# Three of 48 output weight rows spread over eight of the sixteen DMA engines, and score sums over two chunks at a time

## The chip, the cores and the metric

The kernel runs on one core of one Trainium2 chip. The metric is the device time of one execution in microseconds (us). All times below are in us unless they are marked ns. Engines are named as in the profile: PE is the matrix engine (PEld its weight loads), DVE the vector engine, ACT the scalar engine, POOL or GpSimd the general engine, SP the engine that issues most of the transfers. Sixteen DMA engines move the data between HBM and on-chip memory.

## What is computed

One decoding step of a transformer block with attention and a gated FFN side by side, for 4 batch rows (D = 640, 32 heads of Dh = 192, a window of W = 2048 of 8192 cached positions, F = 1536), in bf16:

```python
xn = layernorm(x)
q = (xn @ wq).reshape(B, 1, 32, 192)                   # wq: 640 x 6144
k, v = k_cache[:, :, -2048:, :], v_cache[:, :, -2048:, :]
p = softmax(q . k * 192 ** -0.5)
attn = (p . v).reshape(B, 1, 6144) @ wo                # wo: 6144 x 640
ffn = (silu(xn @ w1) * (xn @ w3)) @ w2                 # w1, w3: 640 x 1536; w2: 1536 x 640
out = x + attn + ffn
```

The windows of the two caches are 201 MB of the 223 MB that are read.

## The kernel before

The 128 partitions hold 32 heads times R = 4 groups of positions. Each batch row has 4 units of 512 positions, and each unit of keys or values is one load of 6,144 KB (`load`, 48 KB in each partition) into one of three `kv` buffers. All large loads are issued by SP in program order; each waits until the buffer that it overwrites is free. `feed` issues the next load of `stream` after each unit of work. Value units of row b alternate with key units of row b + 1.

*A key unit* (`keys`) has NC = 4 chunks of CH = 32 positions. `mult` (L212) multiplies a chunk with the query on DVE into one of two `pr` buffers; `adder` (L219) sums over 12 slices of Dh on PE with 12 matmuls by the identity into a PSUM tile of one bank (`ps_add`, two buffers); `reduces` (L229) sums the last 16 on DVE, one instruction for each chunk, 64 in all. `chain` then makes the softmax weights. *A value unit* (`values`) spreads the weights over heads on DVE (L268) and multiplies with the values in 64 matmuls (L280) into `o_ps` (two buffers). `evict` (L288) and `sort` (L296, L298) bring the result of a batch row into `oT`, with Dh split as 4 x 48: row i of 48 in each partition.

*The end.* wo is used as 48 rows of 640 for each of the 128 partitions (`A_wo.rearrange("(p i) n -> p i n", i=48)`). `wo_load` (L307) loads rows 38 to 47 into a `pr` buffer, then rows 0 to 25 and 26 to 37 into a `kv` buffer, with all partitions at once. `proj` (L315) makes two matmuls for each row, all into one accumulator `acc`: first rows 38 to 47, then 0 to 37. The weights of the FFN's first half (w1, w3) are loaded and used before; w2 comes last, in three pieces of 8, 3 and 1 rows (`w2_load`, L329), and its 24 matmuls (L423) follow the projection. DVE adds `x_st` (the input, loaded by two tiny GpSimd transfers, L125) and `acc`, then the FFN's result (L426), and two transfers write the output. `ordered` fixes the order of instructions on PE and DVE. PSUM has 8 banks: 2 for `ps_add`, 2 for `ps_o`, 3 for `ps_t` (small results, FFN), 1 for `acc`. `pad` (ALIGN) only shifts the addresses of the tiles behind it.

Of the kernel before, what the change touches and what calls it, by code (L numbers as in the profile page):

```python
# [18 lines left out]
def kernel(  # L19
# [15 lines left out]
    WI: int = 10,  # L35
    WM: int = 26,
    ALIGN: int = 64,
):
# [7 lines left out]
    nc = tc.nc  # L46
# [35 lines left out]
    ps_add = ctx.enter_context(tc.tile_pool(name="ps_add", bufs=2, space=MemoryType.PSUM))  # L82
    ps_o = ctx.enter_context(tc.tile_pool(name="ps_o", bufs=2, space=MemoryType.PSUM))
    ps_t = ctx.enter_context(tc.tile_pool(name="ps_t", bufs=3, space=MemoryType.PSUM))
    ps_acc = ctx.enter_context(tc.tile_pool(name="ps_acc", bufs=1, space=MemoryType.PSUM))
# [35 lines left out]
    nc.gpsimd.memset(x_st[:], 0.0)  # L121

    def x_load():
        for t in range(2):
            nc.gpsimd.dma_start(out=x_st[32 * t:32 * t + B, :], in_=x_rows[:, t * DH:(t + 1) * DH])  # L125
# [8 lines left out]
    for s in range(2):  # L134
        load("k", 0, s)

    idb = const.tile([P, P], BF16, name="idb")
# [18 lines left out]
    for b in range(B):  # L156
        nc.vector.tensor_copy(out=qwin[:, b, at:at + NG * R].rearrange("p (g r) -> p g r", r=R),
                              in_=idf[:, b:P:32].unsqueeze(2).to_broadcast([P, NG, R]))
    oT = const.tile([P, NI, 32], BF16, name="oT")
    nc.gpsimd.memset(oT[:], 0.0)  # L160
# [26 lines left out]
    q_pss = []  # L187
    for k in range(NH // 2):
        pool, tag = (ps_add, "ps") if k < 2 else (ps_o, "o_ps")
        qp = pool.tile([P, 512], FP32, tag=tag)  # L190
        q_pss.append(qp)
    for kc in range(KC):
# [8 lines left out]
    for b in range(B):  # L201
        bp = ps_t.tile([P, Dh], FP32, tag="t")
        for k in range(NH):
            w0 = (NH - 1 - k) * NG * R
            pe(nc.tensor.matmul(bp[:], lhsT=qwin[:, b, w0:w0 + P], rhs=q_sb[:, k, :], start=(k == 0), stop=(k == NH - 1)))  # L205
        nc.scalar.copy(out=qb[:, b, :], in_=bp[:])

    scs, es, rss, rcps, pend = {}, {}, {}, {}, []

    def mult(b, s, c):  # L210
# [3 lines left out]
        return pr  # L214

    def adder(b, s, c, pr):
        ps = ps_add.tile([P, CH, DD], FP32, tag="ps")
        for kk in range(NK):
            pe(nc.tensor.matmul(ps[:], lhsT=idb[:], rhs=pr[:, :, kk * DD:(kk + 1) * DD], start=(kk == 0), stop=(kk == NK - 1)))  # L219
        pend.append((b, s, c, ps))  # L220

    def reduces():
        while pend:
            b, s, c, ps = pend.pop(0)
            if b not in scs:
                sc = small.tile([P, NU * NJ], FP32, tag="sc", bufs=1)
                scs[b] = sc
            at = s * NJ + c * CH
            dve(nc.vector.tensor_reduce(out=scs[b][:, at:at + CH], in_=ps[:], axis=AX.X, op=ALU.add))  # L229

# [123 lines left out]

    proj0, proj1 = NI - WI, NI - WI - 1

    def last_values():
        for g in range(VS):
            load("v", B - 1, NU - 1, g * NJ // VS, (g + 1) * NJ // VS)
        wo_load((NI - WI, NI), ppool, "pr", [P, WI, D])  # L360

# [4 lines left out]
    def last_weights():  # L366
        wo_load((0, WM, NI - WI), kvpool, "kv", [P, NJ, Dh])
        for i0, i1 in ((0, (NF - 1) * CF), ((NF - 1) * CF, NF * CF - 1), (NF * CF - 1, NF * CF)):
            w2_load(i0, i1)
# [5 lines left out]
    stream = [(load, u) for u in units[2:-1]] + [(gates, ()), (last_values, ()), (last_weights, ())]  # L375

    def feed():
        fn, args = stream.pop(0)
        fn(*args)

    feed()
# [28 lines left out]
    sort(B - 1)  # L410
    proj(NI - WI, NI)
    proj(0, NI - WI)

# [45 lines left out]
```

## Time and profile before

| | us |
|---|---|
| median of 3 runs | 526.01 (525.87 to 526.31) |
| the profiled execution | 526.01 |
| its span in the profile | 524.08 |
| one unit of keys or values, issue to landing (median) | 28.2 / 27.3 |
| DVE product of one chunk, L212 x64 | 3.351 each, 213.4 in all |
| DVE sum of one chunk, L229 x64 | 0.687 each, 43.9 in all |
| PE adder, L219 x768 | 194.1 in all |
| PE values, L280 x1024 | 115.1 in all |
| PE projection, L315 x96 | 9.5 in all |
| DMA | 223.26 MB, 426 GB/s in the mean |

A page shows one profiled execution: busy time of each engine, its share in 40 slices of the span, the DMA queues, the chain of work that ended last, and the costliest groups of instructions. "L219 PE" is line 219 on PE; "out<-in" are the kernel's tile names. Packets of the trace are pieces that one DMA engine moves as a whole: q1 is the queue of SP's transfers, q0 that of GpSimd's, q8 and q14 are instruction fetches. Behind each engine's part of a transfer stands a completion packet of 4 bytes.

### The profile page before, as it was taken

The page shows a single profiled execution, that of the slowest core. Times are in us where ns is not written, and L with a number is a line of the kernel's source. Part 1 is how long each engine was busy: PE and PEld are TensorE (multiplying, and loading weights), DVE is VectorE, ACT ScalarE, POOL GpSimd, SP SyncE. Part 2 cuts the span into 40 slices and gives each one's busy share as a digit, 9 for nine tenths or more (in the row PEclk, how much of TensorE's full clock was granted, in tenths as well). Part 3 has the DMA queues.
Part 4 walks back from the last instruction along what each step waited for, and adds up shares of the span by engine and source line. Part 5 has one row for each costly group of instructions (what it writes and reads, how often), then busy time and mean ns, then how long its engine had stood idle before and what let it go on. Part 6 is the DMA issues. An engine that isn't in the chain of part 4 may idle for free.

```text
span 524.1 us, 4690 instructions
## 1 busy us (share of the span) xinstructions
PE 341.9 (65%) x2147; PEld 199.4 (38%) x2147; DVE 300.5 (57%) x189; ACT 17.8 (3%) x34; POOL 4.7 (1%) x13
## 2 busy tenths in 40 slices
PE   0507677667676776596675866686565867688447
PEld 0302233253524352363434342353324353475445
DVE  4018999876583937676564828675574839411200
ACT  2110000000000000000000000000000000001100
POOL 3000000000000000000000000000000000000000
PEclk9977999979897887889798887998797888888797
DMA  9999999999999999999999999999999999999995
GB/s 361 431 448 439 420 425 447 439 421 424 436 450 425 420 435 451 431 418 439 443 433 424 424 455 431 425 420 450 436 431 421 435 448 428 428 420 427 432 425 240
DMA packets 6299, 223.26 MB, mean 426 GB/s; under 512 B 756, under 2 KB 904, under 8 KB 1032
## 3 DMA queue, kind: packets, MB, share of 16 engines
q1 hardware_dynamic: 6200, 222.96, 98.6%
q8 instruction: 16, 0.26, 0.2%
q14 instruction: 3, 0.02, 0.0%
q0 software_dynamic: 64, 0.01, 0.0%
q10 hardware_dynamic: 16, 0.01, 0.0%
HBM read 222.96 MB, written 0.01 MB: 425 GB/s over the span
## 4 chain that ended last, share of the span: by engine, by line
DMA 43%; DVE 29%; PE 25%; issue 1%; ACT 1%; SPq 0%; DVEq 0%; ACTq 0%
DMA kv<-in_A_k_cache_dram 38%; DVE pr L212 21%; PE o_ps L280 12%; PE ps L219 9%; DMA wt<-in_A_wo_dram 6%; DVE z L268 4%; DVE sc L229 4%; PE acc L315 2%; PE fp L296 1%; ACT e L252 1%; PE ft L423 0%; PE mt L247 0%; DVE gmax L244 0%; DVE gmq L246 0%; PE mt L242 0%
## 5 line engine op out<-in xcount | busy, mean ns | idle before, releaser
L212 DVE TENSOR_TENSOR pr<-kv,qb 128x6144 bf16<-128x6144 bf16 x64 | 213.4, 3351 | 104.7 <-DMA kv<-in_A_k_cache_dram 104.7
L219 PE MATMUL ps<-pr,idb 128*128 128x512 bf16 x768 | 194.1, 409 | 96.8 <-DVE pr L212 96.8
L219 PEld LDWEIGHTS <-idb 128*128 128x128 bf16 x768 | 79.5, 104 | 208.6 <-issue 122.6
L280 PE MATMUL o_ps<-kv,z 128*64 128x384 bf16 x1024 | 115.1, 396 | 50.6 <-DVE z L268 45.4
L280 PEld LDWEIGHTS <-z 128*64 128x64 bf16 x1024 | 94.5, 197 | 70.6 <-DVE z L268 53.0
L229 DVE TENSOR_REDUCE sc<-ps 128x32 f32<-128x512 f32 x64 | 43.9, 687 | 47.3 <-PE ps L219 47.2
L268 DVE TENSOR_TENSOR z<-e,selz 128x4096 bf16<-128x4096 bf16 (+1 forms) x17 | 36.7, 2158 | 18.2 <-PE o_ps L280 14.5
L315 PE MATMUL acc<-wt,oT 128*32 128x320 bf16 x96 | 9.5, 371 | 6.7 <-DMA wt<-in_A_wo_dram 6.1
L415 DVE CAST t<-acc 64x320 bf16<-64x320 f32 x1 | 0.5, 483 | 22.3 <-PE acc L315 22.3
L288 ACT COPY o_ev<-o_ps 128x384 f32<-128x384 f32 x4 | 1.9, 479 | 289.5 <-PE o_ps L280 289.5
L196 PE MATMUL qp<-wq,xnT 128*32 128x384 bf16 x80 | 5.2, 440 | 7.9 <-DMA wq<-in_A_wq_dram 7.9
L315 PEld LDWEIGHTS <-oT 128*32 128x32 bf16 x96 | 6.5, 118 | 9.5 <-issue 7.0
L296 PEld LDWEIGHTS fp<-o_ev,esel 128*128 128x128 f32 x64 | 7.7, 192 | 1.3 <-ACT o_ev L288 0.9
L296 PE MATMUL fp<-o_ev,esel 128*128 128x48 f32 x64 | 7.6, 272 | 0.6 <-ACT o_ev L288 0.6
L344 DVE TENSOR_TENSOR t_bf<-sg,t_bf 96x512 bf16<-96x512 bf16 x1 | 0.4, 420 | 11.5 <-ACT t_bf L338 11.5
L180 PE MATMUL xnT_ps<-idb,scratch 4*128 4x4 bf16 x5 | 0.4, 178 | 9.9 <-DVE scratch L176 9.9
L196 PEld LDWEIGHTS <-xnT 128*32 128x32 bf16 x80 | 3.1, 128 | 9.8 <-issue 7.5
L252 ACT ACTIVATE e<-sc,negm 128x512 bf16<-128x512 f32 x4 | 2.9, 721 | 80.5 <-DVE negm L249 80.5
L259 DVE RECIPROCAL rcp<-tb 128x1 f32<-128x1 f32 x4 | 0.6, 160 | 7.4 <-PE tb L257 7.4
L298 ACT ACTIVATE oT<-fp,rcp 128x48 bf16<-128x48 f32 x4 | 1.9, 468 | 64.9 <-PE fp L296 64.9
L180 PEld LDWEIGHTS <-scratch 4*128 4x128 bf16 x5 | 0.3, 125 | 9.9 <-DVE scratch L176 9.9
L205 PE MATMUL bp<-scratch 128*128 128x192 bf16 x32 | 3.3, 245 | 0.3
(60 smaller groups left out, 48.1 us busy)
## 6 DMA issues: line engine op xcount, KB each, us to landing
kv<-in_A_k_cache_dram SPq DMA_DIRECT2D x16, 6144.0 KB, 28.2
kv<-in_A_v_cache_dram SPq DMA_DIRECT2D x15, 6144.0 KB, 27.3
wq<-in_A_wq_dram SPq DMA_DIRECT2D x1, 6144.0 KB, 17.4
kv<-in_A_v_cache_dram SPq DMA_DIRECT2D x2, 3072.0 KB
wt<-in_A_wo_dram SPq DMA_DIRECT2D x1, 4160.0 KB, 29.4
ft<-in_B_w_dram SPq DMA_DIRECT2D x2, 1920.0 KB, 18.2
wt<-in_A_wo_dram SPq DMA_DIRECT2D x1, 1920.0 KB
wt<-in_A_wo_dram SPq DMA_DIRECT2D x1, 1600.0 KB, 27.8
```

Source lines behind the costliest of these rows:

```text
L196: pe(nc.tensor.matmul(q_pss[k][32 * g:32 * g + 32, 0:QW], lhsT=xnT[:, kc, :], rhs=wq[:, 2 * k:2 * k + 2, g, :], start=(kc == 0), stop=(kc ...
L205: pe(nc.tensor.matmul(bp[:], lhsT=qwin[:, b, w0:w0 + P], rhs=q_sb[:, k, :], start=(k == 0), stop=(k == NH - 1)))
L212: dve(nc.vector.tensor_tensor(out=pr[:], in0=kvs["k", b, s][:, c * CH:(c + 1) * CH, :], in1=qb[:, b, :].unsqueeze(1).to_broadcast([P, CH, ...
L219: pe(nc.tensor.matmul(ps[:], lhsT=idb[:], rhs=pr[:, :, kk * DD:(kk + 1) * DD], start=(kk == 0), stop=(kk == NK - 1)))
L229: dve(nc.vector.tensor_reduce(out=scs[b][:, at:at + CH], in_=ps[:], axis=AX.X, op=ALU.add))
L252: nc.scalar.activation(out=e[:], in_=sc[:], func=ACTF.Exp, bias=negm[:, 0:1], scale=SCALE, accum_out=rs[:])
L268: dve(nc.vector.tensor_tensor(out=z[:].rearrange("p h (a j) -> p h a j", j=ZB), in0=es[b][:, at:at + n].rearrange("p (a j) -> p a j", j=ZB ...
L280: pe(nc.tensor.matmul(o_pss[b][64 * t:64 * t + 64, 0:2 * Dh], lhsT=zf[:, a:a + (2 * H - 1) * half + 1:half], rhs=vt[:, n0 + a:n0 + a + hal ...
L288: nc.scalar.copy(out=o_ev[:].rearrange("p t d -> p (t d)"), in_=o_pss.pop(b)[:, 0:2 * Dh])
L296: pe(nc.tensor.matmul(fp[:], lhsT=esel[:, t, R - 1 - c:R - 1 - c + P], rhs=o_ev[:, t, c * NI:(c + 1) * NI], start=(c == 0 and t == 0), sto ...
L298: nc.scalar.mul(out=oT[:, :, b:b + 1].rearrange("p i o -> p (i o)"), in_=fp[:], mul=rcps.pop(b)[:, 0:1])
L315: pe(nc.tensor.matmul(acc[32 * t:32 * t + 32, :], lhsT=oT[:, i, :], rhs=wos[i][:, t * DH:(t + 1) * DH], start=(i == i0 and i0 == proj0), s ...
```

## The change

WX = 3 of the 48 wo rows, 45 to 47, leave the common loads. They go into a tile of their own, `wx`, which is zeroed by GpSimd at the start. In `wx`, partitions 0 to 15 and 32 to 47 (of the lower half) and 80 to 95 and 112 to 127 (of the upper half) take the rows of two partitions each, their own and those of a partition 16 away; the other partitions stay zero. There are 16 loads of 4 partitions x 2 x 3,840 bytes. Eight, for the lower half, are issued by SP, one after each of eight unit loads (`feed`). Eight, for the upper half, are issued by GpSimd after the last copy of the query (`qcopy`), each behind a transfer `turn` of 12 partitions x 2 x 16 bytes whose data is not used. The first dimension of a row load is 4 and that of a turn is 12, by which each goes over as many DMA engines.

`proj_ends` computes with these rows: two matmuls by the constant `swap` put each partition's `oT` columns, its own and the other's, side by side (`xp`), ACT copies them to `oX`, and 12 matmuls add to `acc`. It stands between the projection of rows 35 to 44 and that of rows 0 to 34. The pieces of wo become rows 35 to 44, 0 to 22 and 23 to 34.

The adder's PSUM tile holds two chunks (two banks, two buffers), and `reduces` sums two chunks with one instruction, 32 in all. For these banks `ps_o` has one buffer instead of two and `ps_t` two instead of three. The query's four accumulators lie in two adder tiles. ALIGN is 192.

```diff
...
     CH: int = 32,
     R: int = 4,
     WI: int = 10,
-    WM: int = 26,
-    ALIGN: int = 64,
+    WM: int = 23,
+    WX: int = 3,
+    ALIGN: int = 192,
 ):
 
 
...
     opool = ctx.enter_context(tc.tile_pool(name="o", bufs=1))
     small = ctx.enter_context(tc.tile_pool(name="small", bufs=2))
     ps_add = ctx.enter_context(tc.tile_pool(name="ps_add", bufs=2, space=MemoryType.PSUM))
-    ps_o = ctx.enter_context(tc.tile_pool(name="ps_o", bufs=2, space=MemoryType.PSUM))
-    ps_t = ctx.enter_context(tc.tile_pool(name="ps_t", bufs=3, space=MemoryType.PSUM))
+    ps_o = ctx.enter_context(tc.tile_pool(name="ps_o", bufs=1, space=MemoryType.PSUM))
+    ps_t = ctx.enter_context(tc.tile_pool(name="ps_t", bufs=2, space=MemoryType.PSUM))
     ps_acc = ctx.enter_context(tc.tile_pool(name="ps_acc", bufs=1, space=MemoryType.PSUM))
 
     ORDER_DEP = mybir.DependencyInfo(mybir.DependencyClass.NoSync, mybir.DependencyReason.SCHED_ONLY)
...
     x_st = const.tile([64, DH], BF16, name="x_st")
     nc.gpsimd.memset(x_st[:], 0.0)
 
+    wx = const.tile([P, 2, WX * D], BF16, name="wx")
+    nc.gpsimd.memset(wx[:], 0.0)
+    wo_ends = A_wo.rearrange("(p i) n -> p i n", i=NI)[:, NI - WX:NI, :].rearrange("(y x h e q) i n -> y x q e h (i n)", y=2, x=2, h=2, e=4)
+    wx_rows = wx[:].rearrange("(y x h e q) h2 n -> y x h q e h2 n", y=2, x=2, h=2, e=4)
+
+    def wx_load(y, x, q, queue):
+        return queue.dma_start(out=wx_rows[y, x, y, q], in_=wo_ends[y, x, q])
+
     def x_load():
         for t in range(2):
             nc.gpsimd.dma_start(out=x_st[32 * t:32 * t + B, :], in_=x_rows[:, t * DH:(t + 1) * DH])
...
     nc.sync.dma_start(out=wq1[:], in_=wq_rows[:, RV:KC, :])
     for s in range(2):
         load("k", 0, s)
-
     idb = const.tile([P, P], BF16, name="idb")
     make_identity(nc, idb[:])
     idf = const.tile([P, P], FP32, name="idf")
...
     for b in range(B):
         nc.vector.tensor_copy(out=qwin[:, b, at:at + NG * R].rearrange("p (g r) -> p g r", r=R),
                               in_=idf[:, b:P:32].unsqueeze(2).to_broadcast([P, NG, R]))
+    swap = const.tile([P, 2, 4, 2, 16], BF16, name="swap")
+    for h in range(2):
+        nc.gpsimd.tensor_copy(out=swap[:, h], in_=idb[:].rearrange("p (a h r) -> p a h r", a=4, h=2)[:, :, h:h + 1, :].to_broadcast([P, 4, 2, 16]))
     oT = const.tile([P, NI, 32], BF16, name="oT")
     nc.gpsimd.memset(oT[:], 0.0)
 
...
     acc = ps_acc.tile([64, DH], FP32, name="acc")
 
     q_pss = []
-    for k in range(NH // 2):
-        pool, tag = (ps_add, "ps") if k < 2 else (ps_o, "o_ps")
-        qp = pool.tile([P, 512], FP32, tag=tag)
-        q_pss.append(qp)
+    for k in range(0, NH // 2, 2):
+        qp = ps_add.tile([P, 2, 512], FP32, tag="ps")
+        q_pss += [qp[:, 0, :], qp[:, 1, :]]
     for kc in range(KC):
         wq = (wq0[:, kc, :] if kc < RV else wq1[:, 0, :]).rearrange("p (k g d) -> p k g d", g=NG, d=Dh)
         for k in range(NH // 2):
...
         for k in range(NH):
             w0 = (NH - 1 - k) * NG * R
             pe(nc.tensor.matmul(bp[:], lhsT=qwin[:, b, w0:w0 + P], rhs=q_sb[:, k, :], start=(k == 0), stop=(k == NH - 1)))
-        nc.scalar.copy(out=qb[:, b, :], in_=bp[:])
+        qcopy = nc.scalar.copy(out=qb[:, b, :], in_=bp[:])
+    turn = const.tile([12, 8, 2, 8], BF16, name="turn")
+    behind_q = mybir.DependencyInfo(mybir.DependencyClass.Sync, mybir.DependencyReason.SCHED_ONLY)
+    for x in range(2):
+        for q in range(4):
+            di = ordered("pool", nc.gpsimd.dma_start(out=turn[:, 4 * x + q],
+                                                     in_=A_wo.rearrange("(p i) n -> p i n", i=NI)[0:12, 4 * x + q:4 * x + q + 2, 0:8]))
+            if x == 0 and q == 0:
+                tc.add_manual_dep(di.ins, qcopy.ins.name, behind_q, reason="behind the short runs of the query weights")
+            ordered("pool", wx_load(1, x, q, nc.gpsimd))
 
     scs, es, rss, rcps, pend = {}, {}, {}, {}, []
 
...
                                     in1=qb[:, b, :].unsqueeze(1).to_broadcast([P, CH, Dh]), op=ALU.mult))
         return pr
 
+    adds = {}
+
     def adder(b, s, c, pr):
-        ps = ps_add.tile([P, CH, DD], FP32, tag="ps")
+        if c % 2 == 0:
+            ps = ps_add.tile([P, 2, CH, DD], FP32, tag="ps")
+            adds[b, s] = ps
+        ps = adds[b, s]
         for kk in range(NK):
-            pe(nc.tensor.matmul(ps[:], lhsT=idb[:], rhs=pr[:, :, kk * DD:(kk + 1) * DD], start=(kk == 0), stop=(kk == NK - 1)))
-        pend.append((b, s, c, ps))
+            pe(nc.tensor.matmul(ps[:, c % 2], lhsT=idb[:], rhs=pr[:, :, kk * DD:(kk + 1) * DD], start=(kk == 0), stop=(kk == NK - 1)))
+        if c % 2 == 1:
+            pend.append((b, s, c - 1, ps))
 
     def reduces():
         while pend:
...
                 sc = small.tile([P, NU * NJ], FP32, tag="sc", bufs=1)
                 scs[b] = sc
             at = s * NJ + c * CH
-            dve(nc.vector.tensor_reduce(out=scs[b][:, at:at + CH], in_=ps[:], axis=AX.X, op=ALU.add))
+            dve(nc.vector.tensor_reduce(out=scs[b][:, at:at + 2 * CH], in_=ps[:].rearrange("p a j d -> p (a j) d"), axis=AX.X, op=ALU.add))
 
     def keys(b, s):
         for c in range(NC):
...
             pe(nc.tensor.transpose(out=hT_ps[:, c, :], in_=ffn["h"][0:32 * NF, c:NCH:CF], identity=idb[0:32 * NF, 0:32 * NF]))
         dve(nc.vector.tensor_copy(out=hT[:], in_=hT_ps[:]))
 
-    proj0, proj1 = NI - WI, NI - WI - 1
+    NM = NI - WX
+    oX = const.tile([P, 2, WX, 32], BF16, name="oX")
+
+    def proj_ends():
+        xp = ps_t.tile([P, 2, WX * 32], FP32, tag="t")
+        for o in range(2):
+            pe(nc.tensor.matmul(xp[:, o, :], lhsT=swap[:, o].rearrange("p a h r -> p (a h r)"),
+                                rhs=oT[:, NM:NI, :].rearrange("p i o -> p (i o)"), start=True, stop=True))
+        nc.scalar.copy(out=oX[:].rearrange("p o i b -> p (o i b)"), in_=xp[:].rearrange("p o n -> p (o n)"))
+        for o in range(2):
+            for i in range(WX):
+                for t in range(2):
+                    at = i * D + t * DH
+                    pe(nc.tensor.matmul(acc[32 * t:32 * t + 32, :], lhsT=oX[:, o, i, :], rhs=wx[:, o, at:at + DH],
+                                        start=False, stop=False))
+
+    proj0, proj1 = NM - WI, NM - WI - 1
 
     def last_values():
         for g in range(VS):
             load("v", B - 1, NU - 1, g * NJ // VS, (g + 1) * NJ // VS)
-        wo_load((NI - WI, NI), ppool, "pr", [P, WI, D])
+        wo_load((NM - WI, NM), ppool, "pr", [P, WI, D])
 
     def gates():
         ffn_load(1)
         ffn_load(3)
 
     def last_weights():
-        wo_load((0, WM, NI - WI), kvpool, "kv", [P, NJ, Dh])
+        wo_load((0, WM, NM - WI), kvpool, "kv", [P, NJ, Dh])
         for i0, i1 in ((0, (NF - 1) * CF), ((NF - 1) * CF, NF * CF - 1), (NF * CF - 1, NF * CF)):
             w2_load(i0, i1)
 
...
             units += [("v", b, s)] + ([("k", b + 1, s)] if b < B - 1 else [])
     stream = [(load, u) for u in units[2:-1]] + [(gates, ()), (last_values, ()), (last_weights, ())]
 
+    ends = [(0, x, q, nc.sync) for x in range(2) for q in range(4)]
+
     def feed():
         fn, args = stream.pop(0)
         fn(*args)
+        if ends and len(stream) < len(units) - NU:
+            wx_load(*ends.pop(0))
 
     feed()
     for which, b, s in units[:-1]:
...
         values(B - 1, NU - 1, g * NJ // VS, (g + 1) * NJ // VS)
     evict(B - 1)
     sort(B - 1)
-    proj(NI - WI, NI)
-    proj(0, NI - WI)
+    proj(NM - WI, NM)
+    proj_ends()
+    proj(0, NM - WI)
 
     t1 = opool.tile([64, DH], BF16, tag="t1")
     dve(nc.vector.tensor_copy(out=t1[:], in_=acc[:]))
```

## The prediction

> **What bounds the kernel now.** I read the page from its first three parts to the chain, then the end of the chain in order of time, the granted clock around the end, and last the single packet records of the trace.
>
> ```profile
> span 524.1 us, 4690 instructions
> PE 341.9 (65%) x2147; PEld 199.4 (38%) x2147; DVE 300.5 (57%) x189; ACT 17.8 (3%) x34; POOL 4.7 (1%) x13
> DMA  9999999999999999999999999999999999999995
> q1 hardware_dynamic: 6200, 222.96, 98.6%
> q8 instruction: 16, 0.26, 0.2%
> q14 instruction: 3, 0.02, 0.0%
> ```
>
> No compute engine is over 65% busy, and the sixteen DMA engines are over 90% busy in every slice but the last. So the kernel is its transfers, plus what follows the last of them. The last two lines matter more than their shares say: they are instruction fetches, and they use the same engines.
>
> ```profile
> 482.04 29.37 DMA wt<-in_A_wo_dram
> 511.41 0.04 issue
> 511.45 7.95 PE acc L315 x76
> 519.40 1.64 PE ft L423 x24
> 521.05 0.02 issue
> 521.07 0.48 DVE res L426
> ```
>
> This is the end of the chain: rows 0 to 25 of wo land at 511.41, then 76 projection and 24 FFN matmuls run, then the sum and the output transfer. The 29.37 us are the queue, not one transfer.
>
> ```profile
> 505.40:511.45 6.05, 0.00 (x0) 0.00 (x0) 0.00 (x0) 0.00 (x0) 0.00 (x0) 0.88 0.95 410
> 511.45:516.87 5.42, 5.42 (x42) 3.53 (x43) 0.00 (x0) 0.00 (x0) 0.00 (x0) 0.51 0.99 418
> 516.87:519.40 2.53, 2.53 (x42) 2.03 (x40) 0.00 (x0) 0.00 (x0) 0.00 (x0) 1.00 0.56 231
> ```
>
> Stretches of the end (columns: PE, weight loads, DVE, ACT, POOL, then granted clock, DMA share, GB/s). PE is idle for 6.05 us, then works at half clock (about 135 ns a matmul) until 516.87 and at full clock (about 68 ns) after it. The DMA share falls to 0.56 while PE works: some engines are finished, others are not.
>
> The packet records have no engine number, but a stream of packets keeps its phase to a nanosecond from one 6.3 MB load to the next (14.50 us each), so sixteen streams can be told apart by their completion packets. When the 26-row piece completes, measured from the first stream, seven streams lie at 0 to 0.85 us, one at 2.48, and eight at 2.94 to 3.68. All sixteen began within 0.89 of each other. Each of the sixteen 16 KB fetches (q8) set one stream back by 1.42; they go round eight streams, twice each, which makes 2.84. Two 8 KB fetches (q14, at 90.3 and 435.5) set one other stream back by 0.84 each. The kernel thus waits for eight engines that fetch PE's program.
>
> **Part by part.** *Three wo rows.* Now each engine carries 8 partitions of them, 8 x 3,840 bytes. A 3,840-byte packet takes 0.146 from start to start, the same bytes inside the long packets 0.142. The change spares all engines 8 x 0.142 = 1.13 in the 26-row piece and gives eight of them 16 x 0.146 = 2.33 earlier: eight are relieved by 1.13, eight loaded by 1.20 net. It gains only if the relieved eight are the late ones. Evidence: the two tiny x_st transfers of the kernel before (4 partitions) both put their data on the same four streams, and none of these four is one of the late eight. I take these for the lowest four, where the SP loads then go; that the other four loaded ones are early too is the change's own claim.
>
> *The tiny transfers and GpSimd's completions.* Eight of each. An x_st transfer left 4 data packets and 28 of 4 bytes: 16 completions and a filler on each of the 12 engines without data. So per engine I count at most 2 data and 1 completion packet for a turn, and 1 filler and 1 completion for a row load, 40 in all. A 4-byte packet of x_st moved its neighbour by about 7 ns, a 640-byte one by 29. Bounds: 40 x 7 = 0.28, and 16 x 29 + 24 x 7 = 0.63; not below 0, as packets are only added. I take 0.28, since 16-byte runs are nearest to the 4-byte packets.
>
> *DVE sums of two chunks.* 64 reduces of 687 ns become 32 of twice the elements, 1.25 to 1.37: up to 4 us of DVE, off the path. What counts is the 32 instructions fewer. DVE had started 52 instruction records at the first 8 KB fetch and 184 at the second, and no other engine advanced by about 128 between them, so these are DVE's own. It has 213 in all; with 181 the second fetch lies past the end. That stream gets 0.84 back. It is one of the four x_st streams, so it needs this.
>
> [...]
>
> *Work hidden.* Zeroing wx on GpSimd: oT's 1,536 columns took 1.37, so 3,840 take 3.4, ahead of the identities. That moves the normalisation chain by 3.4, and xnT is ready at 10.5 while PE waits for wq until 18.18; uncovered it would cost those 3.4. The swap copies stand behind. GpSimd's 16 issues (0.60 each) wait for ACT's last qb copy at 27.3 and, from the fourth turn on, for earlier transfers; only x_st was in that queue, and it goes first. SP issues 8 more (about 0.42 each), each behind its step's key or value load; a load lands 28 after its issue and takes 14.5, so 13 us of cover. Their completion-semaphore waits are for transfers four steps back. One o_ps buffer instead of two: evict comes a whole key step before the next use. Two transpose banks instead of three: ffn's hT waits for one ACT copy (0.57), inside the idle time before the last values. Two-bank adder tiles keep two in flight; DVE's wait for PE (47.2 over 23 times) only changes place.
>
> *The end.* proj_ends adds 2 + 12 matmuls and one ACT copy (nearest row 0.47) to the 6.05 us idle stretch: about 2.5 with waits, nothing on the path. After the landing 70 matmuls remain, not 76.
>
> **The sum.** Latest stream before: 3.68. After: the late eight 3.68 - 1.13 + 0.28 = 2.83. The early seven at most 0.85 + 1.20 + 0.28 = 2.33. The DVE-fetch stream began at 0.80, near the top of the spread of starts; if it does again it comes to 2.48 - 0.84 + 1.20 + 0.28 = 3.12, from the middle of the starts (0.44) to 2.76. I take the middle, as nothing ties a start to an engine. The landing is then earlier by 3.68 - 2.83 = 0.85, and the projection's long run starts at 511.45 - 0.85 = 510.60. With the clock as before, the 6.27 us to 516.87 hold 46.4 matmuls of 0.135, and the other 23.6 take 1.60 at 0.068: projection ends at 518.47 and FFN, 1.64 later, at 520.11, not 521.04: 0.93. The other limit is the last piece of w2, completed at 520.36 before: FFN's last pair could then not have ended before 520.77 (0.26 until PE sees it, 0.15 for the pair), 0.28 ahead of its actual end. This limit moves by 0.28 + 0.85 = 1.13 and does not bind. The profiled run took 526.01 (span 524.08 and 1.93 around it), which is also the median: 526.01 - 0.93 = 525.1.
>
> Ends: with the start at 0.80 the landing gains 0.56 and the end 0.78; with 0.63 of small packets besides, 0.5; with none of them and w2 as the limit, 0.28 + 1.13 = 1.4. So 524.6 to 525.6 for this case.
>
> [...]
>
> **Rivals.** *Slower: GpSimd's loads land on the same four engines as SP's.* For it: the two x_st transfers came one behind the other and used the same four streams, so a four-engine transfer did not move the next one on. Then the tiny transfer turns nothing, and four engines carry 32 packets, 4.67 - 1.13 = 3.54 net. An early engine becomes the latest from an extra of 3.68 - 0.44 - 0.84 - 0.28 = 2.12 on. The DVE-fetch stream would come to 5.10 to 5.46, 1.42 to 1.78 later than now, and the w2 limit, 0.28 off, makes the end 1.1 to 1.5 later: 527.2 to 527.5. Against it: x_st is two-dimensional and wx is not, so another division may hold.
>
> [...]
>
> *Slower: the other four loaded engines are among the late eight.* Nothing in the records numbers them. Then 3.68 + 1.20 + 0.28 = 5.16, 1.48 later, the end 1.2 later: 527.2.
>
> *No change: DVE's second fetch stays.* The stream comes to 3.60 to 3.96; the end gains at most 0.4: 525.8. Against it: the margin is three records, 181 against 184.
>
> **Chances.** Forecast 0.60; GpSimd's loads on SP's four 0.17; late engines loaded 0.08; fetch stays 0.05; something not seen 0.10 (0.05 faster, 0.01 same, 0.04 slower). What a measurement of this kernel can tell from no change is about 0.2%, 1.05 us, or 524.96; the forecast lies on this edge. A full clock and fewer small packets would take it over, a late start of one stream would not, so its 0.60 splits into 0.33 and 0.27. Faster 0.33 + 0.05 = 0.38, same 0.27 + 0.05 + 0.01 = 0.33, slower 0.17 + 0.08 + 0.04 = 0.29. The range must take in the first slower rival to hold 8 in 10: 524.5 to 527.5; the forecast's own is 524.6 to 525.6.
>
> **What would show it.** Right: two 8 KB fetches during the span become one; the late eight end about 0.9 earlier and the early ones 1.4 later, so the spread at the end shrinks from 3.7 to under 3; the projection's long run has 70 matmuls and starts near 510.6. Wrong: 3,840-byte packets of GpSimd's queue on the streams that also carry SP's; a stream later than 3.7; a gap between loads in any stream; PE or DVE as releaser of the last transfers.

## The result and the profile after

The changed kernel takes 527.36 us in the median (527.06 to 527.68), beside 526.18 (525.85 to 526.44) for the kernel before on the same chip: ratio 1.0023, with an interval of 1.0014 to 1.0031. It is 1.2 us slower, just over what can be told from no change, and inside the range (524.5 to 527.5) but on the other side of the forecast of 525.1. The profiled execution took 527.15, its span 525.4.

From the page of the kernel after (busy time, DMA share in slices, DMA queues):

```profile
span 525.4 us, 4723 instructions
PE 336.9 (64%) x2155; PEld 197.4 (38%) x2155; DVE 298.4 (57%) x157; ACT 18.2 (3%) x35; POOL 17.9 (3%) x32
DMA  8999999999999999999999999999999999999994
q1 hardware_dynamic: 6296, 222.71, 98.3%
q8 instruction: 17, 0.28, 0.2%
q0 software_dynamic: 576, 0.26, 0.2%
q14 instruction: 3, 0.02, 0.0%
```

The kernel is still its transfers: no compute engine is over 64%, and the DMA share is full until the last slice. DVE has 32 listed instructions fewer, as planned, but q14 still has its three packets: the second 8 KB fetch, which was to fall away, is still there. q0 now carries the eight GpSimd loads and the turns.

The end of the chain of waits:

```profile
483.79 36.56 DMA ft<-in_B_w_dram
520.35 0.04 issue
520.39 1.97 PE ft L469 x24
522.36 0.02 issue
522.38 0.48 DVE res L472
```

Where before the long load of wo was released into PE, the chain now goes straight from w2 (`ft<-in_B_w_dram`) to the last 24 matmuls. PE of the same end (start, busy time, tiles, and the idle time ahead with what ended it):

```profile
509.25 0.26 PE L386 MATMUL xp<-oT,swap 128*128 128x96 bf16 x2
509.91 0.99 PE L393 MATMUL acc<-wx,oX 128*32 128x320 bf16 x12 [0.41 <-ACT oX L388]
512.82 3.30 PE L340 MATMUL acc<-wt,oT 128*32 128x320 bf16 x46 [1.91 <-DMA wt<-in_A_wo_dram]
517.34 1.81 PE L340 MATMUL acc<-wt,oT 128*32 128x320 bf16 x24 [1.22 <-DMA wt<-in_A_wo_dram]
520.39 1.95 PE L469 MATMUL ft<-ft,hT 128*32 128x320 bf16 x24 [1.24 <-DMA ft<-in_B_w_dram]
```

The `proj_ends` matmuls run in what was idle time. Then PE waits three times, each time for DMA: for each piece of wo and for w2. The long run starts at 512.82, not at the predicted 510.60. The FFN starts at 520.39 where it started at 519.40 before and ends at 522.36 where it ended at 521.05: 1.31 later, which is the lengthening of the span (525.4 against 524.1). Stretches of this end, in the columns of the prediction:

```profile
511.00:516.87 5.87, 3.30 (x46) 2.59 (x46) 0.00 (x0) 0.00 (x0) 0.00 (x0) 1.00 0.95 404
516.87:520.39 3.52, 1.81 (x25) 1.26 (x24) 0.80 (x2) 0.00 (x0) 0.00 (x0) 1.00 0.49 201
```

The clock is full (1.00) where it was 0.51 in the kernel before, and PE has idle time all the same. In the second stretch the DMA share is 0.49: the DMA engines finish one after another, and PE waits for the last of them.

*Which streams are late.* The sixteen streams of packets, told apart by their phase as in the prediction, in the completion of the 23-row piece. They are counted from where the first stream stood (506.64) until DVE's second fetch, at 480.5, set it back by 0.59:

| group of streams after | us |
|---|---|
| relieved, no PE fetch: three | 0.24, 0.44, 0.59 (the one with that fetch) |
| relieved, two PE fetches each: five | 2.57 to 3.18 |
| SP's four, no PE fetch: three | 2.19, 2.54, 2.55 |
| SP's four, one 8 KB fetch: one | 3.73 |
| GpSimd's four, no PE fetch: one | 2.87 |
| GpSimd's four, two PE fetches each: three | 5.32, 5.51, 5.81 |

GpSimd's eight loads all went to one set of four streams, SP's eight to another. The two pieces of 3,840 bytes that a load brings into a partition of `wx` lie behind each other there. In GpSimd's queue they travel as one packet of 7,680 bytes (32 of them in q0), in SP's as two of 3,840 (64 more in q1 than before): 8 x 0.305 = 2.44 on each of GpSimd's four, 8 x 0.297 = 2.38 on each of SP's. Three of GpSimd's four are streams that also carry two of PE's fetches, 2 x 1.42 = 2.84. Together 5.28, which with starts of 0 to 0.5 is the bottom row. Before, the latest was at 3.68. By the clock of the profile the last stream completes the piece at 512.45, before at 511.09: 1.37 later. The last piece of w2 was complete at 520.3 of the span before and at 521.7 after.

So the loads went where the code sends them, but three of the eight loaded engines are engines that were late.

### The profile page after: what moved, and what is told of

Same layout as the page of the kernel before. It is cut to its first block, busy times and chain, and to the rows that moved or that the text cites. A ratio compares the mean times of both kernels' runs of the same rounds, so it can differ in the third digit from the quotient of the medians.

```text
span 525.4 us, 4723 instructions
## 1 busy us (share of the span) xinstructions
PE 336.9 (64%) x2155; PEld 197.4 (38%) x2155; DVE 298.4 (57%) x157; ACT 18.2 (3%) x35; POOL 17.9 (3%) x32
## 4 chain that ended last, share of the span: by engine, by line
DMA 46%; DVE 29%; PE 21%; issue 3%; ACT 1%; SPq 0%; DVEq 0%; ACTq 0%
DMA kv<-in_A_k_cache_dram 39%; DVE pr L231 20%; PE o_ps L305 12%; PE ps L243 8%; DMA ft<-in_B_w_dram 7%; DVE z L293 4%; DVE sc L254 4%; ACT e L277 1%; DVE lmax L265 1%; PE ft L469 0%; PE mt L272 0%; DVE gmax L269 0%; PE mt L267 0%; DVE gmq L271 0%; SPq L332 0%
## 5 line engine op out<-in xcount | busy, mean ns | idle before, releaser
L231 DVE TENSOR_TENSOR pr<-kv,qb 128x6144 bf16<-128x6144 bf16 x64 | 212.8, 3354 | 115.7 <-DMA kv<-in_A_k_cache_dram 101.5
L243 PE MATMUL ps<-pr,idb 128*128 128x512 bf16 x768 | 190.1, 403 | 95.5 <-DVE pr L231 95.5
L243 PEld LDWEIGHTS <-idb 128*128 128x128 bf16 x768 | 77.6, 102 | 205.2 <-issue 78.5
L254 DVE TENSOR_REDUCE sc<-ps 128x64 f32<-128x1024 f32 x32 | 39.1, 1222 | 36.9 <-PE ps L243 36.9
L340 PE MATMUL acc<-wt,oT 128*32 128x320 bf16 x90 | 6.6, 299 | 3.8 <-DMA wt<-in_A_wo_dram 3.1
L191 PE MATMUL xnT_ps<-idb,scratch 4*128 4x4 bf16 x5 | 0.4, 178 | 13.3 <-DVE scratch L187 13.3
L340 PEld LDWEIGHTS <-oT 128*32 128x32 bf16 x90 | 5.0, 96 | 5.2 <-issue 4.3
L221 POOL DMA_DIRECT2D turn<-in_A_wo_dram x8 | 4.6, 571 | 29.5 <-ACT qb L216 18.6
L191 PEld LDWEIGHTS <-scratch 4*128 4x128 bf16 x5 | 0.3, 125 | 13.3 <-DVE scratch L187 13.3
L130 POOL DMA_DIRECT2D wx<-in_A_wo_dram x8 | 4.7, 582 | 10.4 <-DMA wx<-in_A_wo_dram 10.4
```

Of the source, the lines that this page charges most:

```text
L130: return queue.dma_start(out=wx_rows[y, x, y, q], in_=wo_ends[y, x, q])
L221: di = ordered("pool", nc.gpsimd.dma_start(out=turn[:, 4 * x + q], in_=A_wo.rearrange("(p i) n -> p i n", i=NI)[0:12, 4 * x + q:4 * x + q ...
L231: dve(nc.vector.tensor_tensor(out=pr[:], in0=kvs["k", b, s][:, c * CH:(c + 1) * CH, :], in1=qb[:, b, :].unsqueeze(1).to_broadcast([P, CH, ...
L243: pe(nc.tensor.matmul(ps[:, c % 2], lhsT=idb[:], rhs=pr[:, :, kk * DD:(kk + 1) * DD], start=(kk == 0), stop=(kk == NK - 1)))
L254: dve(nc.vector.tensor_reduce(out=scs[b][:, at:at + 2 * CH], in_=ps[:].rearrange("p a j d -> p (a j) d"), axis=AX.X, op=ALU.add))
L340: pe(nc.tensor.matmul(acc[32 * t:32 * t + 32, :], lhsT=oT[:, i, :], rhs=wos[i][:, t * DH:(t + 1) * DH], start=(i == i0 and i0 == proj0), s ...
```

## The experiments

The question at first: did the time go to the engines that were chosen (the second slower rival), to the turns and GpSimd's completions, or to the two-chunk sums? Ratios are to the kernel before, run on the same chip.

**The sums alone.** The DMA part is left out; the sums over two chunks and their PSUM banks stay.

```diff
-    WM: int = 23,
+    WM: int = 26,
...
-    NM = NI - WX
+    NM = NI
...
-    ends = [(0, x, q, nc.sync) for x in range(2) for q in range(4)]
+    ends = []
...
-    proj_ends()
```

> Only the sums of two chunks with their PSUM buffers; wo is loaded as in the kernel before (26, 12 and 10 rows). Theory A: the streams end as in the kernel before (3.7), time within 0.3 of it, 525.9 to 526.5; both 8 KB fetches of the DVE stream stay in the span, as DVE has 16 more semaphore instructions for 32 fewer sums. A rival that puts the loss on DVE or PSUM waits: about 527.4.

525.97, ratio 0.9999 (0.9989 to 1.0008), and the latest stream at 3.68 as before. The sums over two chunks, the PSUM banks taken for them and the zeroing cost and bring nothing that can be measured. The loss is in what this kernel leaves out: the loads with their turns, and `proj_ends`, which stands in idle time.

**No turns.** The eight `turn` transfers are removed, the rest stays.

> The changed kernel without the tiny transfers of 12 partitions. Theory A (the row loads of GpSimd end on four streams of which three also carry PE's program fetches, and these are the latest): without the turns each GpSimd load of four engines moves on by four, so every stream gets two of the 7,680-byte packets (0.61 us) instead of eight on four streams; program-fetch streams end at 3.7 - 1.13 + 0.61 + 0.15 = 3.3 after the first, the stream of the 8 KB fetches, which also carries SP's loads, at 4.1 to 4.5 and is the latest; time 526.3 to 526.8. Theory B (GpSimd's way of issuing, the small packets, is what costs, wherever the rows go): half of the GpSimd transfers are gone, time about half way back, 526.8, with the spread of the streams as in the changed kernel. Theory C (the order of streams does not follow the turns): all eight loads stay on one set of four streams, 527.2 or more.

527.66, ratio 1.0027 (1.0016 to 1.0039). The 32 packets of 7,680 bytes are on all sixteen streams: without the turn each transfer of four engines moves on by four. The first slower rival, that a turn turns nothing and GpSimd's loads fall on SP's four, is refuted by this and by the packets of the kernel after: its eight turns left 96 packets of 32 bytes, 12 each, its eight GpSimd row loads 32 of 7,680 bytes, 4 each, and the first load lies on the four streams on which the turn ahead of it put no data. The rival was built on the two x_st transfers, which both left their data on the same four streams; why those two did not move on is not shown. The sharing out was better (the streams end within 3.67 of each other), yet the time was not the better one that had been expected, as even the first stream completes only at 509.01 (506.89 in the changed kernel). In 30 to 60 us, while GpSimd's loads run, the DMA engines moved 411 GB/s, where the kernel before moved 434. This run alone does not say why.

This run also numbers the engines. As the loads move on from group to group, the streams of PE's fetches can be placed: taking SP's four as 0 to 3, two of 4 to 7, three of 8 to 11 and three of 12 to 15 carry fetches, none of 0 to 3. GpSimd's four in the changed kernel are then 12 to 15, three of them late.

**Loads on engines that fetch less, three ways.** First, all 16 loads by GpSimd with other turns, of 8 bytes a row here and in the runs with `turn_by` below, aimed at engines 15, 0 to 2 and 3 to 6 (a first series of 3, 4 and 8, then 8 after each pair):

```diff
+    for at, n in enumerate((3, 4, 8)):
+        di = turn_by(n, 8 + at)
...
-            ordered("pool", wx_load(1, x, q, nc.gpsimd))
+            for y in range(2):
+                ordered("pool", wx_load(y, x, q, nc.gpsimd))
+            turn_by(8, 4 * x + q)
```

> All 16 row loads go through GpSimd; turns of 3, 4 and 8 partitions once at the start and one of 8 after each pair of loads place them, if a cursor counts engines, on engines 15, 0, 1, 2 and on 3 to 6, and the turns of 8 on 7 to 14. Theory A: these eight loaded streams carry no program fetch (that fits the records if the fetches lie on 7 to 14), so the late eight are relieved to 2.8, the stream of the 8 KB fetches ends at 3.7 to 4.0 and is the latest; time 526.0 to 526.4, a microsecond or more below the changed kernel. Theory B: twice as many row loads through GpSimd, time 527.9 or more. Theory C: all loads on one set of four streams, over 528.

529.21, ratio 1.0063 (1.0048 to 1.0078): a miss, and worse than the change itself. Two of 4 to 6 carry fetches (streams at 4.98 and 5.02), and from 45 to 105 us DMA moved 417 GB/s instead of 432.

Second, all 16 loads by SP, without turns, so that only the four engines without fetches are loaded, twice as much:

> All 16 row loads go through SP, none through GpSimd, no turns. Theory A: all lie on the same four streams, none with program fetches, each with 4.76 of packets; the stream of the 8 KB fetches ends at 0.44 to 0.8 + 1.68 + 4.76 - 1.13 = 5.7 to 6.1 and is the latest, the late eight at 2.6; time about 527.9 to 528.2. Theory B: no GpSimd transfer is left, time 526.2 or less. Theory C gives the same as A.

529.61, ratio 1.0067 (1.0052 to 1.0082). Loading only four engines doubly is no way out, as expected, but it came out 1.4 over the expected range. Third, one extra turn of 3 engines in front, so that GpSimd's loads fall on 15 and 0 to 2:

```diff
+    di = turn_by(3, 8)
```

> The changed kernel with one more tiny transfer, of 3 partitions, ahead of all: the cursor that places GpSimd's transfers stands 3 engines further, so its row loads should lie on engines 15, 0, 1 and 2 instead of 12 to 15 (the turns of 12, here of 8 bytes a row, on 3 to 14). The number of transfers is as before but for one. Theory A (three of engines 12 to 14 carry program fetches and are loaded besides): the fetch streams are relieved; engines 0 to 2 are loaded twice (SP's and GpSimd's) and end at 3.9 to 4.8 by the first stream of the kernel before, against 4.9 measured for the latest now; time 526.2 to 527.1, below the changed kernel's 527.36. Theory B (the amount that GpSimd issues is what costs): 527.4 as the changed kernel. A theory that double load on any engine is what costs: over 528.

528.39, ratio 1.0043 (1.003 to 1.0056), over the expected 526.2 to 527.1. The packets were placed as planned: three of SP's four streams carry both sets (4.6 to 4.8 from the first stream in the unit loads), the streams with fetches carry none. But even the first stream completes the 23-row piece 2.07 later than in the changed kernel, and from 45 to 105 us DMA moved 416 GB/s. So in all these kernels a second cost had come in, one that struck engines without a single added byte.

**The second cost: whose partitions are written.** In the kernel after, GpSimd's loads write partitions 80 to 95 and 112 to 127 from engines 12 to 15 and DMA moves 432 GB/s beside them; written from 15 and 0 to 2 the same partitions came with 416. So the pairing of engine and partition is suspect. No packet record says which partitions an engine writes, in the large loads or in others, so the test starts from the two pairings of the kernel after, which have no such cost: SP's four, 0 to 3, with partitions 0 to 15 and 32 to 47, and GpSimd's four, 12 to 15, with 80 to 95 and 112 to 127. Partitions so paired are called "own" below, and moving the loads to other engines without moving the destination makes them "foreign". That 4 to 7 have 16 to 31 and 48 to 63, next behind the partitions of 0 to 3, is an assumption. Theory P of the expectations is that the pairing sets the cost. Two kernels test it. Both have an extra turn of 8 in front, which puts GpSimd's loads on 4 to 7. The first keeps their destination (partitions 80 to 95, 112 to 127), the second takes 16 to 31 and 48 to 63, those assumed to be own, with swap matrices to match.

```diff
+    di = turn_by(8, 8)
...
```

> As the run before, but the first tiny transfer has 8 partitions, so GpSimd's row loads should lie on engines 4 to 7. By the streams of the two runs with other placements, two of these carry program fetches. Theory A: these two end at 4.5 to 5.2 and are the latest, time 527.0 to 527.6, as the changed kernel. Theory B: 527.4 too; the profile tells them apart by the streams that carry both the 7,680-byte packets and the fetches, two instead of three.

```diff
+    di = turn_by(8, 8)
...
-        return queue.dma_start(out=wx_rows[y, x, y, q], in_=wo_ends[y, x, q])
+        return queue.dma_start(out=wx_rows[0, x, y, q], in_=wo_ends[y, x, q])
```

> [...] Theory P: the long packets beside the GpSimd loads are back at 1.815 (they were longer by 37 us in sum), so all streams end 2 us earlier, and the time is 527.0 to 527.6, set by the two streams with fetches and loads. Without theory P: 528.8 as before.

528.8, ratio 1.0053 (1.004 to 1.0065) against 526.71, ratio 1.0013 (1.0004 to 1.0022); both were expected at 527.0 to 527.6. Same engines, same bytes, same turns; 2.1 us come back by the destination and the swap matrices that go with it. The stretch in which the loads run, first with the foreign partitions, then with their own, last the kernel after:

```profile
45.00:105.00 60.00, 41.56 (x183) 17.51 (x180) 55.45 (x23) 0.00 (x0) 3.44 (x6) 1.00 1.00 414
```

```profile
45.00:105.00 60.00, 42.18 (x185) 17.80 (x183) 55.81 (x24) 0.00 (x0) 3.43 (x6) 1.00 1.01 435
```

```profile
45.00:105.00 60.00, 42.35 (x184) 17.71 (x182) 55.72 (x24) 0.00 (x0) 2.73 (x5) 0.99 1.00 432
```

The last column is the whole of it: 414 against 435 GB/s, with the DMA share at 1.00 and 1.01. The engines are "busy" in both, only slower: the 49,152-byte packets, mostly 1.815 each, take 44.7 over that in sum (34 to 480 us) with the foreign partitions and 7.9 with their own. The difference is 2.3 for each of sixteen engines, and in the 23-row piece the first and the last stream are both 2.11 later. The kernel after, with 432 in this stretch as before, does not pay this: it explains experiments, not the change.

**Less per engine.** One row instead of three (WX = 1, WM = 25), all by SP, with destinations as in the change, half of them foreign to SP's four engines:

```diff
-    WX: int = 3,
+    WX: int = 1,
...
-    ends = [(0, x, q, nc.sync) for x in range(2) for q in range(4)]
+    ends = [(y, x, q, nc.sync) for x in range(2) for q in range(4) for y in range(2)]
```

> One wo row instead of three is loaded apart, all 16 loads (two partitions' rows of 1,280 bytes to one of four engines) by SP on its four engines, which carry no program fetch; no GpSimd row loads, no turns; rows 37 to 46 and 0 to 36 by the common loads. Theory A: the late eight are relieved by 0.38 to 3.3; SP's four are loaded by 32 packets of 0.055 less 0.38, 1.4, and the one with the 8 KB fetches ends at most at 0.85 + 0.84 + 1.4 = 3.1; the matmuls of proj_ends keep PE's idle time short, so the clock should stay full and the last piece of w2 sets the end: 0.38 + 0.28 less than the kernel before, 525.3 to 525.8. Theory B: no GpSimd row loads, 526 or less as well. If the matmuls and sums added at the end cost by themselves: 526.2 or more.

541.02, from 527.31 to 561.79; the ratio is 1.006 (1.0031 to 1.009) by its two lowest runs alone. The same kernel on another chip:

> The one-row kernel again, unchanged, because its runs spread from 527 to 562 with all streams slow for 200 us. Theory P (an engine that writes partitions which another engine writes in the common loads slows that other one): half of SP's loads do so here, time 525.6 to 526.6 and some long packets over 1.815. Without that effect 525.3 to 525.8. If the spread comes back, the loads of 1,280 bytes cause it.

541.19, from 534.58 to 550.48, ratio 1.0208 (1.0166 to 1.0249) by the two lowest; four of four runs far over any run of the kernel before. So the slowness goes with the kernel and not with one chip, but its size is different in every run. Then the same loads by SP into own partitions alone (0 to 15 and 32 to 47, with four slots in `wx`, four swap matrices and ALIGN 320):

```diff
-        return queue.dma_start(out=wx_rows[y, x, y, q], in_=wo_ends[y, x, q])
+        return queue.dma_start(out=wx_rows[0, x, 0, q][:, 2 * y:2 * y + 2, :], in_=wo_ends[y, x, q])
```

> [...] Theory A (only streams with program fetches are late; what is put on others is free up to their lead): late eight 3.68 - 0.38 = 3.30, SP's four at most 3.1, no long packet slower than 1.815; with the clock full at the end 0.38 + 0.28 less than the kernel before, 525.3 to 525.8. Rival (the added matmuls, transfers or sums cost by themselves): 526.2 or more.

525.66 (ratio 0.9997, 0.9988 to 1.0006). Stretches of 180 us in the middle, foreign partitions first (the profile of the 561.79 run), then own:

```profile
160.00:340.00 180.00, 101.92 (x591) 57.40 (x593) 90.53 (x40) 1.76 (x4) 0.00 (x0) 0.80 1.00 352
```

```profile
160.00:340.00 180.00, 121.12 (x714) 69.51 (x716) 111.00 (x52) 3.52 (x8) 0.00 (x0) 0.86 1.01 435
```

352 against 435 GB/s: in the first the 49,152-byte packets take 2.24 in the mean instead of 1.815, on all sixteen streams. In the second the latest stream is at 3.55 from the first instead of 3.68, and the chain ends with w2 again:

```profile
482.29 36.46 DMA ft<-in_B_w_dram
518.80 2.01 PE ft L464 x24
```

FFN starts 0.60 before that of the kernel before, but now runs 2.01, not 1.64: 520.81 against 521.05. A gain of 0.4 in the medians is within the interval: this is the best placement tried, and its time cannot be told from that of the kernel before.

The change itself with one row (WX = 1, WM = 25, turns and GpSimd's loads kept):

> The changed kernel with one row instead of three apart: SP's four and GpSimd's four engines as there, turns as there. Theory A: the three streams that carry fetches and GpSimd's loads end at 3.68 + 8 x 0.105 - 0.38 + 0.21 = 4.35 and are the latest, 0.67 later than in the kernel before; less 0.28 that the w2 limit has in hand: 526.4 to 526.8, above the one-row kernel that loads SP's four alone. Rival (three rows were simply too many): 525.5 to 525.9, like that kernel.

526.71, ratio 1.0017 (1.0008 to 1.0026), inside the expected range; the three latest streams end 3.8 to 4.0 behind the first (4.1 behind the first stream of the kernel before, where 4.35 was expected). A third of the load costs about half of the loss (0.65 of 1.18 in the medians). The kernel just before it has the same row by SP alone and takes 525.66: the loss goes with the loads that GpSimd puts on engines with fetches.

**What makes the eight engines late.** If it is PE's fetches, fewer PE instructions must make them earlier with the loads of wo untouched. The kernel before, with 11 of the adder's 12 matmuls and every second pair of matmuls of the values left out:

```diff
-        for kk in range(NK):
+        for kk in range(1):
...
-        for j in range(m):
+        for j in range(0, m, 2):
```

> The kernel before with part of PE's work left out, to shorten its program: of the 12 matmuls that sum a chunk only the first is made, and of a value unit's 64 matmuls every second pair; all transfers are the same. PE's program has 1,712 listed instructions instead of 4,144, so 6 or 7 program fetches instead of 16, no stream with more than one. Theory A (the late eight are late by two fetches each): these streams end at most at 0.9 + 1.42 = 2.3, the stream of the 8 KB fetches at about 2.5 is the latest, 1.2 earlier than 3.7; the end comes earlier by 0.5 to 1.5 (half or full clock of PE at the end), 524.6 to 525.6. A theory by which these streams are slow for their place and not for the fetches: spread 3.7 as before, time 525.9 to 526.3.

524.53, ratio 0.9966 (0.9954 to 0.9979), just under the expected range. From its page and its chain:

```profile
span 523.1 us, 2258 instructions
PE 164.0 (31%) x931; PEld 97.0 (19%) x931; DVE 299.5 (57%) x189; ACT 17.9 (3%) x34; POOL 4.7 (1%) x13
q8 instruction: 7, 0.11, 0.1%
```

```profile
478.40 31.76 DMA wt<-in_A_wo_dram
510.15 0.04 issue
510.20 8.24 PE acc L315 x76
518.44 1.64 PE ft L423 x24
```

PE has 931 matmuls and weight loads each instead of 2147, DVE, ACT and POOL have as many instructions as before (189, 34, 13). Seven fetches instead of 16, the latest stream at 2.42 instead of 3.68, and the projection starts at 510.20 instead of 511.45. The first stream completes the piece at 507.41 as before, so the whole gain is in the late ones. The granted clock is lower (0.585 to 0.602 in the mean of a run, beside 0.869 to 0.885 for the kernel before), and the 76 matmuls take 8.24 instead of 7.95, yet the time is the lowest of all: the kernel waits for the fetches of its own program.

**All kernels side by side.** The profiled execution of each: when the first and the last of the sixteen streams complete wo's long piece, what the 49,152-byte packets take over 1.815 in sum (34 to 480 us; about 7 of it stands behind fetches), and the span. "Foreign" marks the kernels in which added loads go into foreign partitions:

| kernel | first stream | last stream | packets over 1.815 | span |
|---|---|---|---|---|
| before | 507.41 | 511.09 | 7.7 | 524.1 |
| after | 506.89 | 512.45 | 7.4 | 525.4 |
| sums alone | 507.45 | 511.13 | 7.1 | 524.1 |
| turn of 8, own partitions | 507.17 | 511.86 | 7.9 | 524.9 |
| one row, SP and GpSimd | 507.52 | 511.50 | 7.5 | 524.4 |
| one row, SP, own partitions | 507.31 | 510.85 | 7.4 | 523.8 |
| less program | 507.41 | 509.83 | 3.1 | 523.1 |
| no turns (foreign) | 509.01 | 512.68 | 33.5 | 525.9 |
| turn of 3 (foreign) | 508.96 | 513.45 | 39.9 | 526.4 |
| turn of 8 (foreign) | 509.28 | 513.97 | 44.7 | 526.9 |
| turns of 3, 4 and 8 (foreign) | 509.22 | 514.23 | 47.0 | 527.2 |
| all by SP (foreign) | 508.62 | 514.52 | 38.9 | 527.7 |
| one row, SP (foreign) | 543.63 | 546.94 | 583.7 | 559.9 |
| the same, another chip | 532.10 | 535.67 | 402.6 | 548.6 |

Every span ends 12.9 to 13.3 after the last stream, whatever the kernel. Two things set that stream: how late all streams are, which goes with the foreign partitions in every row, and how far the last lies behind the first, which goes with fetches and added loads on one engine. The change lost by the second.

## Why the prediction was wrong

*The step that failed* is the sentence "that the other four loaded ones are early too is the change's own claim". The chain of the sum (late eight relieved by 1.13, early eight loaded) rests on it, and nothing in the profile of before supported it: three of GpSimd's four engines carry two of PE's fetches each and became the latest. I gave the opposite case a price of 527.2 and a chance of 0.08; it is what happened, at 527.36. Its mechanism and size were right: it puts the latest stream 5.16 behind the first stream of before (507.41), 1.48 later than the latest of before. Measured are 5.05 and 1.37; with the measured load and small packets the sum gives 3.68 - 1.13 + 2.44 + 0.21 = 5.20. The chance was wrong: four engines out of the twelve left, with eight of the twelve late, gave no reason to think the four early. Three of them were not.

*Sum, term by term.* Load 2.33: measured 2.38 (SP) and 2.44 (GpSimd). Small packets 0.28: measured 0.21 on every stream. The streams, counted from the first stream of before as in the sum: the five relieved late ones end at 1.81 to 2.42, where the sum gives 2.09 to 2.83 for the eight. SP's four without fetches: predicted at most 2.33, measured 1.43 to 1.79. Both are earlier than the sum by a few tenths; that no start is tied to an engine, as the prediction says, leaves this much open.

*DVE's second fetch*, predicted gone, stayed. The count took away the 32 sums (213 to 181 records) but not what came with them: DVE has 16 more semaphore waits (21 to 37), 197 records in all, and the second fetch came when 183 of them had started. The 16 more stand at the product (L231). In the trace of after, 20 products wait for PE, before it was 1; and 16 instructions that wait for DVE's own semaphore alone stand ahead of products, before there was none. The rival "DVE's second fetch stays" put both fetches on one stream of SP's four, at 3.60 to 3.96. Only the first fell there: that stream ends at 2.97 in the sum's count, inside the 2.76 to 3.12 of the sum with one fetch. The second set back a relieved stream, by 0.59. Neither was on the path: GpSimd's three are at least 1.5 later.

*The clock.* Full at the end (1.00): the idle gaps are 1.91, 1.22 and 1.24, and the one of 6.05 with half clock (0.51) behind it is gone. A full clock was one of two things that the prediction's chances counted on to lift the gain over what can be told from no change. The clock did stay full, and it was worth nothing here, as PE then waited for DMA three times and last for w2.

*The turns.* That they take GpSimd's loads to other engines than SP's was an assumption; nothing in the profile of before showed it, and the two x_st transfers spoke against it. It held: GpSimd's eight loads all lie on four streams, and none of these is one of SP's.

*What the cover hid.* Right: the experiment with the sums alone shows no cost of the two-chunk sums, the PSUM banks and the zeroing; `proj_ends` stands in idle time. SP's issues and one-row loads in their own partitions (525.66) show no cost either.

*Which step would have told it.* The numbers were at hand in one respect only: that eight of sixteen streams are late. With SP's four known not to be among them, a random other group of four has on the average 8 / 12 x 4 = 2.7 late ones. With that count behind it the case priced at 527.2 should have been the likeliest.

Left open: why loads into foreign partitions slow all sixteen streams for some 200 us in the one-row kernel, by another amount in each run, and only by 2 to 3 us in the three-row ones. That the destination causes it is shown by one pair of kernels that differ in nothing else but the swap matrices (528.8 and 526.71). The second pair (527.31 at the least, against 525.66) also differs in slots and ALIGN. For the kernels with turns of 3, of 3, 4 and 8, without turns and with all loads by SP it rests on their longer packets, 33.5 to 47.0 in sum against 7.1 to 7.9 in all kernels with own partitions and the whole program; none of them was run with own partitions. Not tried: three rows on engines that are all without fetches, each into its own partitions.

## What to carry to other kernels

This kernel, which is bound by DMA, waited for the slowest of its sixteen engines: in every run the span ends 12.9 to 13.3 us after the last stream. So ask first which engines carry something besides data; here it was the program itself, 16 fetches of 1.42 us on eight of the engines. Before bytes are moved between engines, let a run of the kernel show that the receiving ones are early (three of the eight here were not, and the latest stream came at 512.45 instead of 511.09), and let another show what the pairing of engine and partition costs (528.8 against 526.71 here); the best placement tried, on early engines and in own partitions, could not be told from the kernel before (525.66, ratio 0.9997). Fewer PE instructions (1.25 us earlier start of the projection here, with part of the work left out) were worth more than any sharing out of the last transfers.

## What was not expected of the hardware

- PE's instruction fetches slow this DMA-bound kernel: each set its stream back by 1.42, and with 7 instead of 16 fetches the latest stream goes from 3.68 to 2.42.
- In these kernels small loads into foreign partitions went with a slowing of all sixteen streams: 414 instead of 435 GB/s in one stretch (three rows, GpSimd's queue), 352 instead of 435 for 180 us in another (one row, SP's queue), at a DMA share of 1.00.
- 32 sums fewer on DVE came with 16 semaphore waits more: 197 records, not 181.
